# Second token product written by columns, with x and u turned by DMA, and six norms taken a segment earlier

## The chip, the cores and the metric

The kernel runs on one NeuronCore of one Trainium2 chip. The metric is the device time of one execution in microseconds (us). The unchanged kernel takes 398.41 us in the median of three runs (397.93, 398.41 and 399.13). A smaller number is better.

The core's engines each work through a queue of their own: PE (matrix products; PEld is its loading of the stationary operand), DVE (vector), ACT (scalar functions), POOL (a second, slower vector engine), and SP, which computes nothing and here issues most of the DMA transfers. Engines wait for each other through semaphores.

## The reference

Two layers follow each other. The first is cosine attention over 8 batches, 12 heads, 448 rows and 64 columns per head; the second is an MLP mixer over the attention's output x of shape 8 x 448 x 768.

```
q_n = q / (norm(q) + 1e-6);  k_n = k / (norm(k) + 1e-6)
scores = q_n @ k_n^T / tau
attn   = softmax(scores)                  # over keys
x      = attn @ v, heads side by side     # per batch 448 x 768

h   = relu(x^T @ w_tok1) @ w_tok2         # 768 x 256, then 768 x 448: over the rows (tokens)
u   = x + h^T                             # 448 x 768
h2  = relu(u @ w_ch1) @ w_ch2             # 448 x 1536, then 448 x 768: over the channels
out = u + h2
```

Inputs and output are float32. The kernel multiplies in float16 and accumulates in float32.

## The kernel before

**Tiles and stages.** Two heads form a pair; a batch has 6 pairs and the kernel 48 (0 to 47). A pair is 128 channels of x. The 448 rows of a batch are laid in four windows of 128 (the function windows): even batches use rows 0 to 447 and 64 rows of padding after them, odd batches use the last 128 rows first, so that 64 rows of padding lie in front.

For pair i the stages are: load_qk and load_v bring q, k and v; squares and sums give the sums of squares, norms turns them into 1/(norm + 1e-6) on ACT and DVE, scaled multiplies q and k by it on POOL (tile kq). From pair 12 on tpose_dma turns kq by a DMA transpose into qk; for earlier pairs tpose does this on PE. score multiplies qk (psS, psQ) and takes the exponential on ACT (pt). pv multiplies pt with v into psO, and DVE divides by the row sums into x (128 rows of a window x 4 windows x 128 channels). tok1 is the first token product: x against w1t gives psR, and DVE takes its maximum with 0 into rt (256 tokens by 128 channels). tok2 is the second token product: it gives psU, and DVE adds x to it into u16. udma turns u16 by a DMA transpose into ut, channels on partitions, which the channel products need. m_ch1 multiplies ut with wc1t (psG; relu on ACT into gt), and m_ch2 multiplies gt with wc2t (psF); DVE adds u16 to psF into ost, and SP stores ost.

**Order of the work.** The order is written out by hand. Pairs 0 to 6 have a prologue of their own. From i = 7 to 47 the main loop runs one step for each pair. In step i, PE scores pair i, applies the attention of pair i-1 (pv), takes one unit of channel work, finishes the scores, does tok2 of pair i-2, further units, and tok1 of pair i-1. A unit is one psG or psF group; refill puts a batch's units in a list when its pairs are done, and due spreads them over the steps. After the loop comes a tail with the last two tok2 and all units left.

The function side(i), called in each step after pv, queues the work of the other engines: load_qk six or seven pairs ahead, squares, cast_v, norms, scaled of pair i+2, tpose_dma of pair i+2 and load_v of pair i+4. SP therefore sees, step by step: the loads of q and k, the transpose of qk, the load of v, stores of finished ost tiles, and the transpose of u from tok2. It works them off in that order. For pairs 3 to 17 each pair's norms are taken alone, from pair 18 on three pairs together.

**Buffers.** The PSUM pool ps holds two tiles of tag b (psO, psR, psU and, below pair 12, the transposes of qk); ps2 holds three of tag s (psS, psQ, most psG and psF). x has three buffers, ut two (one for each of two batches in turn), u16 four.

Of the kernel before, what the change touches and what calls it, by code (L numbers as in the profile page):

```python
# [7 lines left out]
FP32 = mybir.dt.float32  # L8
# [14 lines left out]
def kernel(  # L23
# [145 lines left out]
    nc.gpsimd.memset(w1t[0:64, 4, :], 0.0)  # L169
    nc.gpsimd.memset(w2t[:, :, S:S + 64], 0.0)  # L170

# [80 lines left out]
    def sums_of(i):  # L252
        n, col, w = (-1 - i, 0, 1) if i < SINGLE else (i // HP, i % HP, HP)
        h = half.setdefault(n, {})
        if "ssq" not in h:
            tag = "" if w > 1 else "1"
            h["ssq"] = nrm.tile([128, w, 2 * QS], FP32, name=f"ssq_{i}", tag="ssq" + tag, bufs=4)
            h["rn"] = nrm.tile([128, w, 2 * QS], FP32, name=f"rn_{i}", tag="rn" + tag, bufs=4)
        return h, col
# [92 lines left out]
    def pv_rest(i):  # L352
        if old(i):
            return
        st = pipe[i]
        st["x"] = att.tile([128, 4, 128], FP16, name=f"x_{i}", tag="x", bufs=3)
        st["psO"] = [ps.tile([128, 4, E + 2], FP32, name=f"psO_{i}_{hh}", tag="b") for hh in range(2)]
        for m, lo in enumerate(windows(i // NPAIR)):
            for hh in range(2):
                hb = slice(hh * 64, hh * 64 + 64)  # L360
                at = 2 * S * KC + lo
                nc.tensor.matmul(st["psO"][hh][:, m, 0:E + 1], pts[i % 2][hb, at:at + 128],  # L362
                                 vts[(i // HP) % NV][hb, i % HP, 2 * KC, 0:E + 1], start=(m == 0), stop=False)

    def pv(i, hh):
        st = pipe[i]
        vt = vts[(i // HP) % NV]
        if old(i):
            if hh == 0:
                st["x"] = att.tile([128, 4, 128], FP16, name=f"x_{i}", tag="x", bufs=3)  # L370
# [15 lines left out]
    def tok1(i, wide=False):  # L386
# [8 lines left out]
        nc.vector.tensor_scalar_max(out=st["rt"][:], in0=psR[:], scalar1=0.0)  # L395

    def tok2(i, pe=False, wide=False):
        st = pipe[i]
        b, pj = i // NPAIR, i % NPAIR
        if pj == 0:  # L400
            u16[b] = mix.tile([128, DT, 4, 128], FP16, name=f"u16_{b}", tag="u16", bufs=4)
            ut[b] = mix.tile([128, DT, 4, 128], FP16, name=f"ut_{b}", tag="ut")
        psU = (ps2 if wide else ps).tile([128, 4, 128], FP32, name=f"psU_{i}", tag="s" if wide else "b")
        for m, lo in enumerate(windows(b)):
            for tt in range(TT):
                nc.tensor.matmul(psU[:, m], w2t[:, tt, lo:lo + 128], st["rt"][:, tt],  # L406
                                 start=(tt == 0), stop=(tt == TT - 1))
# [91 lines left out]

    SQ_AT = {12: [15, 16], 13: [17], 14: [18, 19], 15: [20]}  # L500
    SU_AT = {15: [18, 19]}

    with tc.manual_schedule():
# [116 lines left out]

        def side(i):
            single = i + 2 < SINGLE
            n = 6 if i < 2 * NPAIR else 7
            for t in range(i + n, i + (8 if i == 2 * NPAIR - 1 else n + 1)):
                if t < NP_ALL:
                    load_qk(t)
            for t in SQ_AT.get(i, [i + 3 if single else i + 5]):
                if t < NP_ALL:  # L630
                    squares(t)
            cast_v(i)
            if i in (8, 10):
# [12 lines left out]
            if i + 4 < NP_ALL:  # L646
                load_v(i + 4)

        for i in range(NPAIR + 1, NP_ALL):
# [39 lines left out]
        tok2(last)  # L689
# [38 lines left out]
```

## Time and profile before

The profiled execution took 395.4 us, of which 393.6 us are the span from its first to its last instruction; the three timed runs have a median of 398.41 us, 3.0 us above it.

| engine | busy us | share of the span | instructions |
|---|---|---|---|
| PE | 375.2 | 95% | 4132 |
| PEld | 243.5 | 62% | 4132 |
| DVE | 210.5 | 53% | 469 |
| ACT | 224.8 | 57% | 378 |
| POOL | 236.0 | 60% | 383 |

| group | count | mean ns of one |
|---|---|---|
| psU, tok2's product, 128 columns | 384 | 219 |
| psG, channel product 1, 448 columns | 576 | 352 |
| u <- psU, x on DVE, 128x512 | 48 | 691 (median) |
| ssq <- sq on DVE, one pair, 128x960 | 36 | 1143 |
| ut <- u, DMA transpose, issue on SP | 45 | 1241 (median) |
| qk <- kq, DMA transpose | 36 | landing 3.4 us after issue (median) |

Matrix products are pipelined: the mean of one contains its way through the array, and what one costs in a row is the distance from one start to the next. SP's rows show how long an issue holds the queue; the transfer itself goes on after it. The page counts SP's instructions as no work, so SP does not stand in the table of engines; it has to be read from the timeline of its queue. DMA queues: 117951 packets, 65.26 MB, q1 (SP) busy 67.6% of 16 engines over the span.

### The profile page before, as it was taken

Reading aid. Unit: us, or ns where it says so; the run is one execution under the profiler, and the core shown is the slowest. Engines: PE = TensorE matmul, PEld = TensorE weight load, DVE = VectorE, ACT = ScalarE, POOL = GpSimd, SP = SyncE. Lnnn points to the kernel's source line nnn. Section 1 sums busy time; section 2 is a strip of 40 time slices with the busy share of each in tenths; the row PEclk is TensorE's granted clock in tenths of the full one; section 3 lists DMA queues with packets and bytes.
Section 4 is the critical chain, followed back from the end, with each engine's and each line's share of the span. In section 5 each row is a group of like instructions: output and inputs, shape, how many; then the busy total and the mean of one; then the engine's idle time right before and its main releaser. Section 6 shows DMA issues by size and latency. Waiting matters only on the chain.

```text
span 393.6 us, 10211 instructions
## 1 busy us (share of the span) xinstructions
PE 375.2 (95%) x4132; PEld 243.5 (62%) x4132; DVE 210.5 (53%) x469; ACT 224.8 (57%) x378; POOL 236.0 (60%) x383
## 2 busy tenths in 40 slices
PE   5899899899999999999999999999999999999994
PEld 5567566476556666667656666667666666655562
DVE  6889767567544574465534574456534653421031
ACT  5899578665574547764574547755575536411400
POOL 6999887889777592939587592949484630000000
PEclk9899999999999999999999999999999999999999
DMA  8999999989787778896897688686786384022022
GB/s 213 260 234 205 243 260 195 219 216 218 177 201 172 156 182 213 161 174 177 176 220 165 156 213 202 159 176 146 183 187 132 91 158 68 15 65 83 0 81 81
DMA packets 117951, 65.26 MB, mean 166 GB/s; under 512 B 75920, under 2 KB 114320, under 8 KB 117904
## 3 DMA queue, kind: packets, MB, share of 16 engines
q1 hardware_dynamic: 113104, 58.71, 67.6%
q0 software_dynamic: 4080, 5.21, 7.7%
q10 hardware_dynamic: 720, 0.69, 0.6%
q8 instruction: 32, 0.52, 0.6%
q14 instruction: 15, 0.12, 0.1%
HBM read 43.45 MB, written 11.01 MB: 138 GB/s over the span
## 4 chain that ended last, share of the span: by engine, by line
PE 79%; POOL 6%; ACT 5%; DVE 5%; issue 2%; DMA 1%; POOLq 0%
PE psF L446 26%; PE psG L431 26%; PE psO L379 8%; PE psS L340 6%; PE psU L406 5%; PE psR L392 4%; ACT pt L341 3%; POOL kq L293 2%; PE psQ L347 2%; POOL sq L241 1%; DVE ssq L264 1%; PE psO L362 1%; POOL w1t L182 1%; DVE ost L450 1%; DMA qk<-kq 1%
## 5 line engine op out<-in xcount | busy, mean ns | idle before, releaser
L341 ACT ACTIVATE pt<-psS 128x896 f16<-128x896 f32 (+1 forms) x156 | 132.5, 917 | 57.8 <-PE psS L340 57.6
L431 PE MATMUL psG<-ut,wc1t 128*128 128x448 f16 x576 | 116.8, 352 | 0.8 <-ACT gt L434 0.8
L446 PE MATMUL psF<-wc2t,gt 128*128 128x384 f16 x672 | 115.9, 326 | 0.2 <-ACT gt L434 0.2
L446 PEld LDWEIGHTS <-gt 128*128 128x128 f16 x672 | 63.6, 98 | 39.0 <-issue 0.3
L434 ACT ACTIVATE gt<-psG 128x448 f16<-128x448 f32 x96 | 51.3, 543 | 60.9 <-PE psG L431 60.9
L293 POOL TENSOR_TENSOR kq<-kf,rn 128x384 f16<-128x384 f32 (+1 forms) x47 | 42.3, 899 | 70.8 <-ACT rn L281 62.0
L431 PEld LDWEIGHTS <-wc1t 128*128 128x128 f16 x576 | 53.9, 98 | 45.4 <-issue 1.1
L450 DVE TENSOR_TENSOR ost<-psF,u 128x384 f32<-128x384 f32 (+1 forms) x64 | 35.5, 554 | 63.6 <-PE psF L446 62.3
L264 DVE TENSOR_REDUCE ssq<-sq 128x15 f32<-128x960 f32 (+2 forms) x49 | 55.7, 1140 | 3.0 <-ACT sq L239 2.9
L395 DVE TENSOR_SCALAR rt<-psR 128x256 f16<-128x256 f32 x48 | 20.2, 420 | 62.6 <-PE psR L392 62.5
L293 POOL TENSOR_TENSOR kq<-qf,rn 112x512 f16<-112x512 f32 x45 | 47.0, 1044 | 3.0
L379 PE MATMUL psO<-vt,pt 128*128 128x65 f16 (+1 forms) x1248 | 48.3, 193 | 0.0
L379 PEld LDWEIGHTS <-pt 128*128 128x128 f16 (+1 forms) x1248 | 42.2, 97 | 5.1 <-issue 1.9
L340 PE MATMUL psS<-qk 64*128 64x448 f16 x312 | 41.3, 358 | 3.5 <-DMA qk<-kq 2.1
L383 DVE TENSOR_TENSOR x<-psO,rec 128x256 f16<-128x256 f32 x96 | 40.8, 425 | 3.3
L241 POOL TENSOR_TENSOR sq<-kf 128x384 f32<-128x384 f32 (+1 forms) x46 | 40.1, 872 | 1.9 <-DVE ssq L264 1.9
L241 POOL TENSOR_TENSOR sq<-qf 112x512 f32<-112x512 f32 x39 | 40.5, 1039 | 0.0
L409 DVE TENSOR_TENSOR u<-psU,x 128x512 f16<-128x512 f32 x48 | 33.0, 688 | 6.0 <-PE psU L406 4.4
L382 DVE RECIPROCAL rec<-psO 128x4 f32<-128x4 f32 x96 | 16.9, 176 | 29.0 <-PE psO L379 29.0
L406 PEld LDWEIGHTS <-w2t 128*128 128x128 f16 x384 | 24.6, 98 | 10.4 <-issue 3.3
L406 PE MATMUL psU<-rt,w2t 128*128 128x128 f16 x384 | 29.4, 219 | 1.7 <-DVE rt L395 1.1
L392 PEld LDWEIGHTS <-w1t 128*128 128x128 f16 x384 | 25.0, 98 | 8.2 <-DVE x L383 1.2
(55 smaller groups left out, 262.2 us busy)
## 6 DMA issues: line engine op xcount, KB each, us to landing
qf<-in_q_dram SPq DMA_DIRECT2D x48, 224.0 KB, 3.9
kf<-in_k_dram SPq DMA_DIRECT2D x36, 192.0 KB, 3.4
vf<-in_v_dram SPq DMA_DIRECT2D x36, 192.0 KB, 3.2
vf<-in_v_dram SPq DMA_DIRECT2D x12, 224.0 KB, 7.8
out_dram<-ost SPq DMA_DIRECT2D x8, 336.0 KB, 3.1
wc1t<-in_moe_w_ch_dram POOLq DMA_DIRECT2D x4, 576.0 KB, 10.2
wc2t<-in_moe_w_ch_dram POOLq DMA_DIRECT2D x2, 1152.0 KB, 10.7
out_dram<-ost SPq DMA_DIRECT2D x8, 288.0 KB, 2.9
```

The lines of the kernel that those rows point to most:

```text
L241: nc.gpsimd.tensor_mul(out=dst, in0=src, in1=src)
L264: nc.vector.tensor_reduce(out=h["ssq"][0:n, col, sl], in_=pipe[i]["sq"][0:n, sl], axis=AXX.X, op=ALU.add)
L293: eng.tensor_tensor(out=kq[0:p, a, 0:n].rearrange("p c g e -> p g c e"), in0=st["kq"[a]][:].rearrange("p (g c) e -> p g c e", g=2), in1=_b ...
L340: nc.tensor.matmul(psS[:, hh, 0:S], qk[hb, c * n:c * n + 128], qm[hb], start=True, stop=True)
L341: nc.scalar.activation(out=pts[i % 2][0:n, 2 * S * c:2 * S * (c + 1)].rearrange("p (h s) -> p h s", h=2), in_=psS[0:n, :, 0:S], func=AF.Ex ...
L379: nc.tensor.matmul(psO[:, m, 0:E + 1], pts[i % 2][0:n, at:at + 128], vt[0:n, i % HP, nch * hh + c, 0:E + 1], start=(old(i) and c == 0), st ...
L383: nc.vector.tensor_tensor(out=st["x"][:, :, hh * E:(hh + 1) * E], in0=psO[:, :, 0:E], in1=_bcast_free(rec[:], E), op=ALU.mult)
L392: nc.tensor.matmul(psR[:, tt], w1t[:, w1[m], tt * 128:(tt + 1) * 128], st["x"][:, m], start=(m == 0), stop=(m == 3))
L406: nc.tensor.matmul(psU[:, m], w2t[:, tt, lo:lo + 128], st["rt"][:, tt], start=(tt == 0), stop=(tt == TT - 1))
L431: nc.tensor.matmul(psG[:, 0:S], wc1t[:, dt, ct * 128:(ct + 1) * 128], ut[b][:, dt].rearrange("p m s -> p (m s)")[:, lo:lo + S], start=(dt ...
L434: nc.scalar.activation(out=gt[:, ct, (b % 2) * S:(b % 2 + 1) * S], in_=psG[:, 0:S], func=AF.Relu)
L446: nc.tensor.matmul(psF[:, 0:DH], gt[:, ct, lo:lo + 128], wc2t[:, ct, dh * DH:(dh + 1) * DH], start=(ct == 0), stop=(ct == CT - 1))
```

## The change

From batch 1 on (pairs 6 to 47, 42 of them) tok2 multiplies the other way round: rt is the stationary operand and all 448 columns of w2t stream past it, two products of 448 columns in place of eight of 128. psU then has channels on partitions, as ut has, so DVE adds and writes straight into ut. For that x must be turned too: the new function xdma turns x into xt by a DMA transpose, issued in side(i) for pair i-1 right after the loads of q and k. The transpose that used to turn u16 into ut now turns ut into u16, which only the last addition reads. ut becomes two fixed tiles, whose 64 columns of padding are set to zero once; w2t gets 64 more columns in front for the odd batches, and place_w2 one more copy. x goes from three buffers to two, ssq and rn of the threefold norms from four to three.

In steps 9 to 14 the sums and norms of pairs 12 to 17 are taken in the step three pairs ahead, after the last scores and before tok2, where they stood in the following step; scaled and tpose_dma of these pairs then stand first in the step's POOL and SP work (after xdma). squares are listed one step earlier to feed this. The tail issues xdma of the last pair and takes one unit more before the last tok2.

```diff
-    w2t = cst.tile([128, TT, S + 64], FP16, name="w2t")
+    w2t = cst.tile([128, TT, S + 128], FP16, name="w2t")
...
     def place_w2():
-        nc.gpsimd.tensor_copy(out=w2t[:, :, 0:S].rearrange("p t (c s) -> p t c s", c=NCH),
-                              in_=w2n[:].rearrange("p t (s c) -> p t c s", c=NCH))
+        w2c = w2n[:].rearrange("p t (s c) -> p t c s", c=NCH)
+        nc.gpsimd.tensor_copy(out=w2t[:, :, 64:S + 64].rearrange("p t (c s) -> p t c s", c=NCH), in_=w2c)
+        nc.gpsimd.tensor_copy(out=w2t[:, :, 0:64], in_=w2c[:, :, NCH - 1, SC - 64:SC])
...
+    uts = [cst.tile([128, DT, 4, 128], FP16, name=f"ut{i}") for i in range(2)]
+    for i in range(2):
+        nc.gpsimd.memset(uts[i][:, :, 3 - 3 * i, 64 - 64 * i:128 - 64 * i], 0.0)
...
+    def xdma(i):
+        st = pipe[i]
+        st["xt"] = att.tile([128, 4, 128], FP16, name=f"xt_{i}", tag="xt", bufs=2)
+        nc.sync.dma_start_transpose(out=st["xt"][:], in_=st["x"][:].rearrange("p m d -> p (m d)"))
...
     def tok2(i, pe=False, wide=False):
...
-            ut[b] = mix.tile([128, DT, 4, 128], FP16, name=f"ut_{b}", tag="ut")
+            ut[b] = uts[b % 2]
+        if i >= NPAIR:
+            lo = 64 * (b % 2)
+            psU = ps.tile([128, 512], FP32, name=f"psU_{i}", tag="b")
+            for tt in range(TT):
+                nc.tensor.matmul(psU[:, 0:S], st["rt"][:, tt], w2t[:, tt, 64 - lo:64 - lo + S],
+                                 start=(tt == 0), stop=(tt == TT - 1))
+            nc.vector.tensor_tensor(out=ut[b][:, pj].rearrange("p m s -> p (m s)")[:, lo:lo + S], in0=psU[:, 0:S],
+                                    in1=st["xt"].rearrange("p m s -> p (m s)")[:, lo:lo + S], op=ALU.add)
+            nc.sync.dma_start_transpose(out=u16[b][:, pj], in_=ut[b][:, pj].rearrange("p m s -> p (m s)"))
+            return
...
-    SQ_AT = {12: [15, 16], 13: [17], 14: [18, 19], 15: [20]}
-    SU_AT = {15: [18, 19]}
+    SQ_AT = {9: [12, 13], 10: [14], 11: [15], 12: [16], 13: [17], 14: [18], 15: [19, 20]}
...
         def side(i):
...
-            for t in SQ_AT.get(i, [i + 3 if single else i + 5]):
+            xdma(i - 1)
+            if i > 9 and single:
+                scaled(i + 2)
+                tpose_dma(i + 2)
+            for t in SQ_AT.get(i, [i + 3 if single else i + 5])[0:1]:
                 if t < NP_ALL:
                     squares(t)
             cast_v(i)
...
-            if single:
+            for t in SQ_AT.get(i, [])[1:]:
+                squares(t)
+            if i < 10:
                 norms(i + 2, i + 3)
                 norms(i + 2, i + 3, dve=True)
-            elif i + 4 < NP_ALL:
+                scaled(i + 2)
+            elif not single and i + 4 < NP_ALL:
...
-            if i + 2 < NP_ALL:
+            if not single and i + 2 < NP_ALL:
                 scaled(i + 2)
-                if i + 2 >= DMA_T0:
-                    tpose_dma(i + 2)
+                tpose_dma(i + 2)
...
                 score_rest(i)
+            if 9 <= i and i + 3 < SINGLE:
+                sums(i + 3)
+                norms(i + 3, i + 4)
+                norms(i + 3, i + 4, dve=True)
             if i > NPAIR + 1:
                 tok2(i - 2)
...
-            if i + 2 < SINGLE:
-                for t in SU_AT.get(i, [i + 3]):
-                    sums(t)
+            if i < 9:
+                sums(i + 3)
+            elif i + 3 == SINGLE:
+                sums(i + 3)
+                sums(i + 4)
...
+        xdma(last)
         tok2(last - 1)
         unit()
         tok1(last)
         unit()
+        unit()
         tok2(last)
```

More of the change, by code (lines that the diff above doesn't have):

```diff
@@ L169 @@
     nc.gpsimd.memset(w1t[0:64, 4, :], 0.0)
-    nc.gpsimd.memset(w2t[:, :, S:S + 64], 0.0)
+    nc.gpsimd.memset(w2t[:, :, S + 64:S + 128], 0.0)
     def weights_tok1():
@@ L256, in sums_of @@
             tag = "" if w > 1 else "1"
-            h["ssq"] = nrm.tile([128, w, 2 * QS], FP32, name=f"ssq_{i}", tag="ssq" + tag, bufs=4)
-            h["rn"] = nrm.tile([128, w, 2 * QS], FP32, name=f"rn_{i}", tag="rn" + tag, bufs=4)
+            h["ssq"] = nrm.tile([128, w, 2 * QS], FP32, name=f"ssq_{i}", tag="ssq" + tag, bufs=3 + (w == 1))
+            h["rn"] = nrm.tile([128, w, 2 * QS], FP32, name=f"rn_{i}", tag="rn" + tag, bufs=3 + (w == 1))
         return h, col
@@ L355, in pv_rest @@
         st = pipe[i]
-        st["x"] = att.tile([128, 4, 128], FP16, name=f"x_{i}", tag="x", bufs=3)
+        st["x"] = att.tile([128, 4, 128], FP16, name=f"x_{i}", tag="x", bufs=2)
         st["psO"] = [ps.tile([128, 4, E + 2], FP32, name=f"psO_{i}_{hh}", tag="b") for hh in range(2)]
@@ L369, in pv @@
             if hh == 0:
-                st["x"] = att.tile([128, 4, 128], FP16, name=f"x_{i}", tag="x", bufs=3)
+                st["x"] = att.tile([128, 4, 128], FP16, name=f"x_{i}", tag="x", bufs=2)
             n, nch = SC, NCH
@@ L405, in tok2 @@
             for tt in range(TT):
-                nc.tensor.matmul(psU[:, m], w2t[:, tt, lo:lo + 128], st["rt"][:, tt],
+                nc.tensor.matmul(psU[:, m], w2t[:, tt, 64 + lo:64 + lo + 128], st["rt"][:, tt],
                                  start=(tt == 0), stop=(tt == TT - 1))
```

## The prediction

> **What bounds the kernel now.** First the page: how busy PE is, and what the chain that ended last consists of.
>
> ```profile
> span 393.6 us, 10211 instructions
> PE 375.2 (95%) x4132; PEld 243.5 (62%) x4132; DVE 210.5 (53%) x469; ACT 224.8 (57%) x378; POOL 236.0 (60%) x383
> PE 79%; POOL 6%; ACT 5%; DVE 5%; issue 2%; DMA 1%; POOLq 0%
> ```
>
> PE sets the pace. Then the chain in order of time over one step in the middle; columns are start, length, engine, tile, line, number.
>
> ```profile
> 203.31 1.14 PE psG L431 x6
> 204.44 0.19 PE psQ L347
> 204.63 0.45 PE psU L406 x8
> 205.08 3.41 PE psG L431 x18
> ```
>
> There is no gap: a psU group of eight 128-column products costs 0.45 us (56 ns each), six products of 448 columns cost 1.14 us (190 ns each). Starts in PE's timeline, compared with these rates, leave only some 5 us of stalls between 46 and 340 us. The largest, 1.9 us, stands before step 12's scores (77.49): PE waits for qk of pair 12, whose transpose was issued at 70.23 and landed 7.2 us later.
>
> What stands next to PE? No page row counts SP, so I read its queue's timeline (start, length of the issue), here with one long wait in it.
>
> ```profile
> 217.91 0.67 SPq L129 DMA_DIRECT2D qf<-in_q_dram  x1
> 218.62 0.50 SPq L111 DMA_DIRECT2D kf<-in_k_dram  x1
> 223.17 1.23 SPq L325 DMA_TRANSPOSE qk<-kq  x1
> 224.45 0.58 SPq L111 DMA_DIRECT2D vf<-in_v_dram  x1
> 225.13 1.20 SPq L415 DMA_TRANSPOSE ut<-u  x1
> 226.42 0.99 SPq L464 DMA_DIRECT2D out_dram<-ost  x2
> 227.47 0.49 SPq L129 DMA_DIRECT2D qf<-in_q_dram  x1
> 228.00 0.49 SPq L111 DMA_DIRECT2D kf<-in_k_dram  x1
> 228.54 1.30 SPq L119 DMA_DIRECT2D kr<-in_k_dram  x2
> 229.94 1.26 SPq L325 DMA_TRANSPOSE qk<-kq  x1
> ```
>
> Issues follow each other with about 0.05 us between; only before the transpose of qk does SP wait (4.05 us here, for POOL's scaled). Summed over 91 to 284 us (steps 14 to 40, the ones that still load q and k): 197 issues last 158.3 us, their small gaps 10.3 us, and twelve waits over 0.3 us make up 24.6 us, of 193. SP is 87% full there. The landing times of the u transposes, in 45 to 64 us and in 91 to 284 us, and the table of stages (DMA share and GB/s are its last columns):
>
> ```profile
> DMA to landing us min/median/max: 6.3/7.7/9.1
> DMA to landing us min/median/max: 2.5/3.1/4.8
> ```
>
> ```profile
> 46.00:82.00 36.00, 33.74 (x407) 21.29 (x408) 22.32 (x57) 26.30 (x46) 28.59 (x43) 1.00 1.17 236
> 91.00:284.00 193.00, 191.50 (x2115) 124.19 (x2114) 105.61 (x226) 115.27 (x193) 135.62 (x225) 1.00 0.81 180
> 330.00:345.00 15.00, 14.30 (x155) 9.00 (x154) 5.17 (x13) 7.05 (x12) 0.00 (x0) 1.00 0.10 19
> ```
>
> The DMA engines are overfull up to 82 us (share 1.17, slow landings), with room after it (0.81).
>
> **What the Trainium skill says.** "TensorE: Matmul & The Clock Gate", section "Wait — 56ns, not 53.3ns?": warm products start N/2.4 GHz + 2.5 ns apart, 55.8 ns for 128 columns and 189 for 448; the trace agrees (56 and 190). "Perfetto Trace Analysis", section "DMA Instruction — HWDGE (DVE, Sync)": the reported time of such a DMA begins when its semaphores are satisfied and ends when the sequencer is free for the next. So SP's rows are occupancy, and waits are the gaps; the 0.05 us between neighbours agree. "DMA: Bandwidth & Descriptors", section "Issuing engines are not separate DMA queues", calls issue time "usually small relative to the DMA itself"; here it is 1.24 of 3.1 us for a u transpose, so I don't use that. "PSUM — Partial Sum Buffer", section "Engine vs sequencer instructions": the vector queue is strictly first in, first out. So a DVE addition that waits for a transfer holds what is behind it.
>
> **The change part by part.**
>
> PE. Two products of 448 columns, 2 x 190 = 380 ns, replace 450 ns: 0.07 us for each of 42 pairs, 2.9 us at most, and only where PE sets the pace. In the 15 steps outside 14 to 40 that is 1.0 us.
>
> DVE. The addition shrinks from 512 to 448 columns (about 0.07 us); DVE is 53% busy: nothing. But it now also waits for xt, and behind it on DVE stand rt, ost of later units and the next x, for which PE waits through PSUM buffers.
>
> SP. The old u transpose is replaced one for one by that of ut into u16, which is needed only much later. xdma is new: 42 issues of the same shape as the u transposes, which take 1.24 us in the median and 1.35 in the mean in 91 to 284 us, plus 0.05 of gap. 27 of them fall there: 27 x 1.29 = 34.8 us, or 27 x 1.40 = 37.8. Even if every wait vanished, SP would lack 34.8 - 24.6 = 10.2 to 13.2 us. What may be late first? The transpose of qk is issued right behind xdma; now it lands (issue + 3.4) 2.2 to 7.2 us, mostly about 4, before its scores. So SP may fall about 4 us behind for nothing, after which each us that it lacks pushes the next score, and PE with it: 6.2 to 9.2 us. PE's saving there is lost in it. I take 7.6 us. Steps 41 to 47 load no q and k; SP has room again, but time lost isn't won back.
>
> DMA engines. In 330 to 345 us a share of 0.10 over 15 us moved 19 GB/s, 285 KB, which is 2.2 transposes of 131 KB: 0.7 us of all 16 engines each. Per step of 7.3 us that is 0.10 of share: 0.81 becomes 0.91, below the 1.17 reached earlier. Taken as nothing; at worst landings grow by 0.5 us, and the free 4 us shrink as much. Before 82 us it is 7 x 0.7 = 5 us more in a full system. xt of pairs 7 and 8, issued as soon as SP is free (53.4 and 61.6 us), would land 7.7 us later, at 61.1 and 69.3; the additions stand at 61.4 and 67.2, or later by the next item. From nothing to 2 us each: I take nothing.
>
> Norms earlier. In steps 9 and 10 sums (1.14), Ln and Exp on ACT (0.32 + 0.22) and the DVE pair (0.19 + 0.25) come before tok2's addition: DVE is free at 61.4 in step 9 now, then at about 63.6, and the addition ends at 64.2 in place of 62.1. The copy of qk for the next step (it is still turned on PE) stands behind it, and psR needs psU's buffer, as the turned qk holds the other. PE would start psR at 62.7 and waits until 64.2: 1.5 us, the same in step 10: +3.0. From step 11 on no qk is turned on PE, and the units behind psU cover the delay. The gain: the transpose of pair 12 goes out some 2 to 3 us earlier, behind xdma of pair 9, which ends the 1.9 us wait: -1.9. Earlier POOL work for pairs 12 to 17 has no price; POOL is 60% busy. The second copy in place_w2 and the memsets (0.2 us each for such shapes) lie beside a prologue that waits for ACT: nothing, at most 0.5.
>
> Tail. PE stalls of about 0.35 us each between 340 and 347.5 us; one more unit (1.1 us) between tok1 and the last tok2 covers one or two: -0.5. xt of the last pair (x at 343.6, landing 2.4 us in this quiet part) comes before its addition.
>
> Sum: -1.0 + 7.6 + 3.0 - 1.9 - 0.5 = +7.2. Profiled: 395.4 + 7.2 = 402.6. The median of the runs stood 3.0 above the profiled execution: 398.4 + 7.2 = 405.6.
>
> **The rivals.**
>
> Faster. SP takes xdma in its stride, because waits and slack give more than I think. The point: 24.6 + 4 = 28.6 us for 27 issues, 1.06 us each. If an xdma costs SP less, PE stays the bound and the change is worth -2.9 - 1.9 - 0.5 + 3.0 = -2.3, down to -5.3 if the delays of steps 9 and 10 don't occur: 393.1 to 396.1, middle 395. For it: waits are long where they occur, and the earlier scaled of pairs 12 to 17 frees SP. Against: even the shortest u transpose took 1.19 us, with a queue idle before it or not.
>
> Slower still. xt comes late and stops DVE. As SP falls behind, xdma of a pair lands one step later than it is wanted: x is ready 2.3 us into a step, the addition 4.35 us into the next, with a lag of 4 us and a landing of 3.1 it comes 1 to 3 us late. If that, and not the score, is what PE feels first, the free 4 us aren't there: 398.4 + 7.2 + 4 = 409.6, and with the early xt (2 x 2) up to 414. It decides once SP's lag at xdma passes some 2 us.
>
> No change. SP's lack is just covered, as by slacks of 7 us and issues of 1.19: 27 x 1.24 - 24.6 - 7 = 1.9, with +3.0 - 1.9 - 0.5 - 1.0: +1.5; 398 to 400.
>
> **How the numbers follow.** SP bound as summed 0.63 (own range 401 to 409.5), slower still 0.15 (409.5 to 415), no change 0.07, faster 0.15. About 0.3% (1.2 us) can be told from no change here. Faster 0.14, same 0.06, slower 0.80. Time 405.6. The range reaches down to 397 and up to 412: it leaves out most of the faster case and half of the slowest, about 0.2.
>
> **What would show it.** Right: SP's waits in 91 to 284 us fall from 24.6 us to a few; steps there lengthen from 7.3 us on average by some 0.3; PE's waits name the transpose of qk, or DVE's addition waits for xt. psU groups take 0.38 us. The stall at step 12 is gone, new ones of 1.5 us stand before psR in steps 9 and 10. Wrong: xdma rows well below 1.2 us, or SP still waiting 5 us every third step, with steps no longer than before.

## The result, and the profile after

The changed kernel takes 418.9 us in the median of four runs (417.32 to 423.15), the kernel before 398.17 us beside it: a ratio of 1.0549, 95% interval 1.0456 to 1.0641. It is slower by some 20.7 us; 405.6 us (397 to 412) were forecast. The sign and the queue were right, the size was not. Executions more than 1.5% above the fastest of their kernel are left out of all medians and ratios of the experiments (e2, e5, e8, e13, e17 and the kernel before have some); with them e2's median is the 400.65 us that a later expectation names.

The profiled execution after is the longest of its four (423.15 us, span 421.4), so its absolute numbers lie some 4 us above the median. Its page first:

```profile
span 421.4 us, 9851 instructions
PE 380.9 (90%) x3880; PEld 234.8 (56%) x3880; DVE 208.5 (49%) x469; ACT 225.4 (53%) x378; POOL 237.4 (56%) x386
PE 67%; DMA 11%; DVE 9%; ACT 5%; POOL 4%; issue 2%; DVEq 0%; POOLq 0%
L422 DVE TENSOR_TENSOR ut<-psU,xt 128x448 f16<-128x448 f32 x42 | 25.9, 617 | 35.3 <-DMA xt<-x 27.9
```

PE fell from 95% to 90% of its span, and from 79% to 67% of the chain that ended last; transfers took 11% of that chain (1% before). The last line is the new addition: 42 of them, 617 ns each, with 35.3 us of idle DVE ahead of them, 27.9 of these until xt landed. The waits over the whole span show three links, DVE waiting for xt, PE for DVE's addition, and PE for qk (columns: us in total, times, longest):

```profile
DVE ut L422 <- DMA xt<-x: 27.9, 13, 5.6
PE psG L454 <- DVE ut L422: 11.7, 8, 3.1
PE psS L346 <- DMA qk<-kq: 6.8, 2, 6.6
```

Between 95 and 330 us PE waits mostly for the addition and hardly for qk:

```profile
PE psG L454 <- DVE ut L422: 10.4, 6, 3.1
PE psS L346 <- DMA qk<-kq: 0.3, 1, 0.3
```

SP's timeline at the place where the kernel before had a hole of 4.05 us (its 217.91 to 229.94):

```profile
207.02 1.24 SPq L331 DMA_TRANSPOSE qk<-kq  x1
208.31 0.57 SPq L111 DMA_DIRECT2D vf<-in_v_dram  x1
208.94 1.26 SPq L119 DMA_DIRECT2D vr<-in_v_dram  x2
210.30 1.01 SPq L487 DMA_DIRECT2D out_dram<-ost  x2
211.41 1.27 SPq L424 DMA_TRANSPOSE u<-ut  x1
212.72 0.58 SPq L129 DMA_DIRECT2D qf<-in_q_dram  x1
213.35 0.45 SPq L111 DMA_DIRECT2D kf<-in_k_dram  x1
213.90 1.19 SPq L406 DMA_TRANSPOSE xt<-x  x1
```

There is no hole. From step 14 to step 41 SP now waits 1.8 us in all (25.3 before, same steps), its issues, as the rows of the timeline give them, fill 202.9 of 218.4 us (164.4 of 200.5 before), and each new transpose took 1.21 us on average. The chain in order of time shows what that does:

```profile
213.90 4.78 DMA xt<-x
...
218.77 0.64 DVE ut L422
219.41 0.04 issue
219.45 4.06 PE psG L454 x12
```

x of that pair was ready 2.6 us into its step; SP came to its transpose only 11.9 us after the step had begun, and it landed at 218.68. The addition had been waiting 4.50 us, with DVE idle as its queue works in order, PE 3.12 us for the buffer that psU held. Then twelve products took 4.06 us, where the same twelve had taken 2.43 us at 213.89. The view by stretches gives the granted clock (third number from the end) during these products and after them:

```profile
219.45:222.80 3.35, 3.35 (x10) 1.32 (x10) 0.00 (x0) 0.54 (x1) 3.18 (x6) 0.50 0.95 276
223.00:225.00 2.00, 2.00 (x35) 1.38 (x34) 0.42 (x1) 1.25 (x2) 1.31 (x3) 1.00 1.12 194
```

The Trainium skill, "TensorE: Matmul & The Clock Gate", Part 1, section "What's actually happening", says that after an idle window of about 3.4 us PE drops to half its clock. This trace agrees on the half clock and not on the length, and the measurement decides: the stall here was 3.12 us, and one of 2.01 us, which ended at 171.49, was followed by a clock of 0.52 over 2.1 us. Three such stretches of some 3.4 us lie between 168 and 320 us. At half clock a stretch costs at most half its length, so they took up to 5 us of this execution (an estimate from these numbers).

Earlier, the chain holds one long transfer:

```profile
72.18 13.20 DMA qk<-kq
85.38 0.05 issue
85.43 1.30 PE psS L346 x6
```

The transpose of qk of pair 12 was to gain from the change. It was issued at 72.18, held SP for 6.28 us by itself (SP's timeline; 1.23 before) and landed 13.2 us after its issue began. PE waited 6.6 us. The change alone doesn't make such an issue: in e14, which adds nothing here, the same transpose held SP for 5.33 us. The stages, and the landings of xt in 45 to 64 and in 95 to 318 us:

```profile
46.00:82.00 36.00, 29.52 (x325) 17.09 (x322) 19.66 (x51) 24.10 (x43) 29.03 (x44) 1.00 1.16 204
95.00:318.00 223.00, 208.00 (x2090) 126.62 (x2086) 110.30 (x237) 123.63 (x208) 147.41 (x244) 0.98 0.88 184
```

```profile
DMA to landing us min/median/max: 8.3/9.0/9.8
DMA to landing us min/median/max: 2.5/3.2/4.8
```

In the late stage the DMA engines had room (share 0.88) and a turned x landed 3.2 us after its issue. It was late because it was issued late.

To find where time is lost I compare when each step begins (its first scores on PE) with the profile of the kernel before, whose steps 7, 11, 14, 16 and 47 begin at 43.68, 70.16, 89.20, 103.95 and 333.78 us. That execution (395.40 us) lies 2.2 to 3.5 us under the medians of its kernel, so the delays come out that much larger than against a median. The labels e1 to e14 are the experiments of the next section. Delays in us, one profiled execution each:

| kernel | median us (before beside it) | step 7 | 11 | 14 | 16 | 47 |
|---|---|---|---|---|---|---|
| changed | 418.9 (398.2) | 0.5 | 3.3 | 10.4 | 12.9 | 28.1 |
| e1 columns only | 419.8 (398.0) | 3.9 | 5.2 | 11.0 | 11.6 | 26.0 |
| e2 norms only | 400.3 (398.0) | 0.1 | 2.1 | 0.6 | 4.8 | 4.8 |
| e3 turned, unread | 415.3 (398.0) | 0.3 | 0.3 | 7.6 | 9.2 | 20.2 |
| e4 v by POOL | 405.1 (398.0) | 3.0 | 6.2 | 8.7 | 12.6 | 11.7 |
| e5 from batch 2 | 409.2 (398.0) | 0.3 | 2.4 | 2.3 | 5.2 | 11.9 |
| e6 wide units | 418.3 (398.0) | -0.2 | 5.3 | 9.0 | 11.3 | 21.5 |
| e7 both cures | 407.1 (398.0) | -0.1 | 2.0 | 6.2 | 8.7 | 12.3 |
| e9 two small copies | 413.2 (397.6) | 0.5 | 0.5 | 5.8 | 6.9 | 17.8 |
| e10 three small copies | 434.3 (397.6) | 0.1 | 0.1 | 6.6 | 10.6 | 38.4 |
| e11 six early, unread | 403.2 (397.6) | 0.0 | 0.5 | 7.3 | 8.0 | 8.0 |
| e13 x last | 427.7 (398.9) | 3.8 | 9.1 | 10.9 | 13.7 | 34.8 |
| e14 memsets | 397.9 (398.9) | 0.3 | 0.3 | 4.1 | 4.3 | 4.2 |

The early columns vary by some 4 us from one execution to the next: e14 changes nothing in steps 11 to 14 and loses 3.9 us there in this one execution. For the early part I therefore lean on medians, for the late one (16 to 47) on both. The traces show where the early variation comes from. PE's stall before step 12 lasted 1.8 to 1.9 us in the kernel before, e12 and e15, and the granted clock stayed at 1.00. In ten profiles it lasted 2.5 us or longer (4.5 in e14, 5.3 in e3, 6.6 in the changed kernel), and in each of them a stretch of 3.4 to 10.2 us at a clock of 0.50 begins in it or right after it.

### The profile page after: what moved, and what is told of

It reads as the page before. It is cut to its first block, busy times and chain, and to the rows that moved or that the text cites. A ratio compares the mean times of both kernels' runs of the same rounds, so it can differ in the third digit from the quotient of the medians.

```text
span 421.4 us, 9851 instructions
## 1 busy us (share of the span) xinstructions
PE 380.9 (90%) x3880; PEld 234.8 (56%) x3880; DVE 208.5 (49%) x469; ACT 225.4 (53%) x378; POOL 237.4 (56%) x386
## 2 busy tenths in 40 slices
DMA packets 140797, 70.74 MB, mean 168 GB/s; under 512 B 98768, under 2 KB 137168, under 8 KB 140752
## 4 chain that ended last, share of the span: by engine, by line
PE 67%; DMA 11%; DVE 9%; ACT 5%; POOL 4%; issue 2%; DVEq 0%; POOLq 0%
PE psF L469 26%; PE psG L454 20%; PE psO L385 7%; DMA xt<-x 6%; PE psS L346 5%; PE psR L398 4%; DMA qk<-kq 3%; ACT pt L347 3%; PE psU L420 3%; DVE ssq L270 2%; DMA w2n<-in_moe_w_tok_dram 2%; DVE ost L473 2%; DVE ut L422 2%; POOL kq L299 1%; PE psO L368 1%
## 5 line engine op out<-in xcount | busy, mean ns | idle before, releaser
L454 PE MATMUL psG<-ut,wc1t 128*128 128x448 f16 x576 | 121.8, 360 | 12.6 <-DVE ut L422 11.7
L454 PEld LDWEIGHTS <-wc1t 128*128 128x128 f16 x576 | 55.6, 99 | 64.8 <-issue 18.7
L469 PEld LDWEIGHTS <-gt 128*128 128x128 f16 x672 | 64.5, 98 | 42.6 <-issue 1.2
L346 PE MATMUL psS<-qk 64*128 64x448 f16 x312 | 42.4, 364 | 9.1 <-DMA qk<-kq 6.8
L401 DVE TENSOR_SCALAR rt<-psR 128x256 f16<-128x256 f32 x48 | 20.2, 420 | 54.3 <-PE psR L398 54.2
L422 DVE TENSOR_TENSOR ut<-psU,xt 128x448 f16<-128x448 f32 x42 | 25.9, 617 | 35.3 <-DMA xt<-x 27.9
L398 PEld LDWEIGHTS <-w1t 128*128 128x128 f16 x384 | 25.9, 100 | 11.0 <-issue 3.7
L398 PE MATMUL psR<-x,w1t 128*128 128x128 f16 x384 | 30.2, 223 | 2.0 <-DVE ut L422 1.9
L354 ACT ACTIVATE pt<-psQ 128x448 f16<-128x448 f32 x36 | 19.4, 539 | 23.1 <-PE psQ L353 23.1
## 6 DMA issues: line engine op xcount, KB each, us to landing
wc1t<-in_moe_w_ch_dram POOLq DMA_DIRECT2D x4, 576.0 KB, 10.6
```

The lines of the kernel that those rows point to most:

```text
L346: nc.tensor.matmul(psS[:, hh, 0:S], qk[hb, c * n:c * n + 128], qm[hb], start=True, stop=True)
L398: nc.tensor.matmul(psR[:, tt], w1t[:, w1[m], tt * 128:(tt + 1) * 128], st["x"][:, m], start=(m == 0), stop=(m == 3))
L454: nc.tensor.matmul(psG[:, 0:S], wc1t[:, dt, ct * 128:(ct + 1) * 128], ut[b][:, dt].rearrange("p m s -> p (m s)")[:, lo:lo + S], start=(dt ...
L469: nc.tensor.matmul(psF[:, 0:DH], gt[:, ct, lo:lo + 128], wc2t[:, ct, dh * DH:(dh + 1) * DH], start=(ct == 0), stop=(ct == CT - 1))
```

## The experiments

**Each half of the change alone.** e1 keeps the columns and the turning and puts the norms back:

```diff
-    SQ_AT = {9: [12, 13], 10: [14], 11: [15], 12: [16], 13: [17], 14: [18], 15: [19, 20]}
+    SQ_AT = {12: [15, 16], 13: [17], 14: [18, 19], 15: [20]}
+    SU_AT = {15: [18, 19]}
...
-            if 9 <= i and i + 3 < SINGLE:
-                sums(i + 3)
-                norms(i + 3, i + 4)
-                norms(i + 3, i + 4, dve=True)
```

> The columns and the turning of x alone, with the norms, sums and transposes of pairs 12 to 17 in the order of the kernel before. If the whole loss comes from the new transposes (first from overfull DMA engines up to step 13, about 8 to 10 us, then from SP's full queue, about 17 us in the profiled execution), this kernel is within 2 us of the changed one: 416 to 421 us. If my prediction's step on the norms holds (+3.0 - 1.9 us), it is some 1 us faster than the changed one. If it is the earlier norms that bring the early loss (their transposes now meet the transposes of x), then it is 6 to 10 us faster than the changed one: 409 to 413 us.

419.75 us, 1.0526 (1.0441 to 1.0610): all of the loss is here. e2 is the opposite, the second token product and u's transposes as before, the norms early.

> The earlier norms alone: the second token product, its additions and the transposes of u are those of the kernel before, x isn't turned. By my prediction's steps: +1.5 us in each of steps 9 and 10, -1.9 us at step 12, +1.1 us in sum: 399 to 400 us. If the early loss comes from the norms: 404 to 408 us. If the earlier transposes only gain: 396 to 397 us.

400.28 us, 1.0056 (1.0025 to 1.0086), 2.3 us more than before; the 1.1 that my steps gave is at the lower end of the interval (1.0 to 3.4 us). In the profile steps 9 and 10 lose 1.4 and 0.7 us (1.5 each were forecast) and the stall at step 12 is gone, 2.0 us, as forecast, but the delay came out again in step 14. PE's timeline of e2 (start, length, idle before and its releaser):

```profile
92.04 0.60 PE L362 MATMUL psO<-vt,pt 64*128 64x65 f16 x8 [1.47 <-DVE u L409]
92.58 0.98 PE L379 MATMUL psO<-vt,pt 128*128 128x65 f16 x24
93.37 3.75 PE L446 MATMUL psF<-wc2t,gt 128*128 128x384 f16 x12
```

u's addition, behind the norms on DVE, still held psU's buffer when the next step's psO wanted it: 1.47 us. Then the twelve psF products took 3.75 us; another such group at 97.59 took 2.11. So the price of this stall was 1.5 + 1.6 us.

**Turned, but read by nobody.** In the kernel before, x is turned at the changed kernel's place into a tile that nothing reads.

```diff
+    def xdma(i):
+        st = pipe[i]
+        st["xt"] = att.tile([128, 4, 128], FP16, name=f"xt_{i}", tag="xt", bufs=2)
+        nc.sync.dma_start_transpose(out=st["xt"][:], in_=st["x"][:].rearrange("p m d -> p (m d)"))
...
+            xdma(i - 1)
             for t in SQ_AT.get(i, [i + 3 if single else i + 5]):
```

(The tile x has two buffers in place of three to make room; so it has in e11 below, which loses nothing after step 16.)

> The kernel before (all of it, rows and norms too), with the transposes of x added at the place where the changed kernel issues them, into a tile that nothing reads (and two buffers of x in place of three). SP and the DMA engines carry the same as in the changed kernel, but no DVE addition waits for xt. Theory of the prediction (SP falls behind, and the transposes of qk come late): the loss is nearly the same, 410 to 419 us. Theory that the lateness of xt, through the DVE addition and the buffer of psU, is what PE feels: the loss up to step 13 stays in part (qk of pair 12 is late with or without a reader, 4 to 6 us), the rest of 17 us is mostly gone: 402 to 408 us.

415.33 us, 1.0421 (1.0342 to 1.0500). 17.3 of the 20.7 us come without a reader, so the reader isn't needed for most of the loss. In the changed kernel SP's lack reaches PE through the addition; without a reader it reaches PE through qk, as the prediction had it. The waits of PE in 95 to 330 us in e3, where the kernel before has no entry of this kind at all:

```profile
PE psS L340 <- DMA qk<-kq: 13.5, 15, 1.6
```

**Relieving SP.** In the changed kernel v is loaded by POOL's queue from pair 11 on:

```diff
-            (nc.scalar if nm == "k" and i < 3 else nc.sync).dma_start(
+            (nc.scalar if nm == "k" and i < 3 else nc.gpsimd if nm == "v" and i > 10 else nc.sync).dma_start(
```

(and likewise the other two loads of v.)

> The changed kernel with the loads of v (from pair 11 on) and its rest rows issued by POOL's queue in place of SP's. That takes some 0.6 us a step (18 to 20 us between steps 14 and 40) from SP, more than the 10 to 13 us which it lacked; the DMA engines carry the same bytes. If SP's queue is the cause of the loss after step 14 (17 us): 402 to 406 us. If the DMA engines' load is the cause: within 2 us of the changed kernel. The stall before step 12 (6.6 us) should stay either way.

405.13 us, 1.0137 (1.0040 to 1.0235): 13.8 us less, with the same bytes. After step 16 nothing is lost any more; the delay falls from 12.6 to 11.7 us. SP's timeline has 21.6 us of waits again in steps 14 to 41. The row of the stage in e4 (98 to 302 us):

```profile
98.00:302.00 204.00, 199.77 (x2035) 123.02 (x2033) 107.48 (x232) 121.12 (x204) 169.96 (x275) 0.99 1.00 196
```

The DMA engines' share is 1.00 there, above the changed kernel's 0.88, and from step 16 on the kernel is still no slower than before. So the late loss is SP's time and not the DMA engines'. The Trainium skill, "DMA: Bandwidth & Descriptors", section "Issuing engines are not separate DMA queues", says that issuing from several engines saves only sequencer time, "usually small relative to the DMA itself". Here that time was worth 13.8 us.

**The dose.** The kernel before, with two or three copies of 4 KB a step where e3 has the transpose of x (the edit is against e3):

```diff
-        nc.sync.dma_start_transpose(out=st["xt"][:], in_=st["x"][:].rearrange("p m d -> p (m d)"))
+        for j in range(2):
+            nc.sync.dma_start(out=st["xt"][0:16, j], in_=st["x"][0:16, j])
```

> The kernel before with two small copies (16 rows of 256 bytes each, of x into a tile that nothing reads) in every step at the place of the transpose of x. They take SP's time and hardly any of the DMA engines'. If each takes SP about 0.5 us as a load of k does, a step has some 1.1 us more on SP, 27 x 1.1 = 30 us against 25 us of waits in steps 14 to 40. If SP's time alone makes the late loss, and the waits and slack of an undisturbed start are really there: 0 to 4 us, 398 to 402 us, SP's waits down to some 5 us. If the early loss is the DMA engines' (as I think), the stage up to step 16 loses under 2 us; if it is SP's there too, 4 us or more and 403 to 408 us.

> The same with three small copies: 27 x 1.6 = 43 us against 25 us of waits, so SP lacks some 18 us in steps 14 to 40. If SP's time alone makes the late loss: 12 to 18 us there, 410 to 416 us, with hardly a wait left on SP and the share of the DMA engines as in the kernel before. If it is what the transposes do in the DMA engines: within 3 us of the kernel before. Early (up to step 16): under 2 us if that loss is the DMA engines', 5 us or more if it is SP's.

413.16 us, 1.0371 (1.0326 to 1.0416), and 434.28 us, 1.0908 (1.0853 to 1.0963). Both lie above every range that I had named, for I had the copies too cheap: a step's two took 1.34 us in the mean, its three 2.1 (27 steps). Summed from SP's timelines over steps 14 to 41, added issues less vanished waits are 38.0 - 24.5 = 13.5 us in e3, 36.1 - 24.0 = 12.1 in e9, about 58 - 24.0 = 34 in e10. The stage grew by 11.1, 12.1 and 30.8 us. The stage rows of the kernel before and of e9 (DMA share and GB/s last):

```profile
89.00:290.00 201.00, 199.34 (x2198) 129.12 (x2199) 109.29 (x232) 120.92 (x204) 140.91 (x236) 1.00 0.81 183
```

```profile
95.00:307.00 212.00, 199.29 (x2186) 128.21 (x2187) 109.05 (x231) 120.44 (x203) 140.71 (x234) 1.00 0.73 170
```

With the DMA engines idler than before (0.73), the loss after step 14 is that of the transposes. What PE waits for in 95 to 330 us, in e9 and in e10:

```profile
PE psS L340 <- DMA qk<-kq: 11.3, 13, 1.5
```

```profile
PE psS L340 <- DMA qk<-kq: 27.2, 17, 3.2
```

**The early transposes.** e5 is the changed kernel with columns from batch 2 on; e11 is e3 with only the six transposes of pairs 6 to 11.

```diff
-        if i >= NPAIR:
+        if i >= 2 * NPAIR:
             lo = 64 * (b % 2)
...
-            xdma(i - 1)
+            if i - 1 >= 2 * NPAIR:
+                xdma(i - 1)
```

> The changed kernel with the columns from batch 2 on: pairs 6 to 11 keep the rows of the kernel before, so the six transposes of x in steps 7 to 12 aren't issued; SP's load after step 13 is unchanged. If these six transposes, in the stage where the DMA engines are overfull, cost the early loss (step 16 starts 12.9 us late in the changed kernel, 4.8 us with the norms alone), 6 to 8 us come back: 411 to 413 us. If SP also enters the later stage less behind, up to 4 more: 407 to 411. If the early loss comes from somewhere else: within 2 us of 418.9.

> The kernel before with the six transposes of x for pairs 6 to 11 alone (steps 7 to 12), read by nothing; no other pair is turned. If these six make the early loss of the unread version (9.2 us by step 16): 404 to 408 us, with no loss after step 16. If that loss needs what follows (the seventh and later transposes, SP's queue): 398 to 401 us.

e5: 409.18 us, 1.0272 (1.0194 to 1.0350), 9.7 us less than the changed kernel. e11: 403.2 us, 1.0117 (1.0065 to 1.0170), 5.6 us more than the kernel before by the medians (2.6 to 6.8 by the interval). These six issues cost about half as much as the other 35 of e3. In e11's profile nothing is lost after step 16. In e5's profile the late stage (step 16 to 47) costs 6.8 us in place of 15.2; in e3's, 11.0.

I expected the small copies to lose under 2 us early if the transposes' own work in the full DMA engines were the reason. They lost 5.8 and 6.6 us by step 14 in their profiles; e14, which adds nothing there, lost 4.1 in its one. By the medians e9 lost 15.6 us, of which 10.9 came after step 16 in its profile, so some 4.7 are left for the early part (an estimate). So it isn't the transposes' work alone. Nor is SP full in this stage: in steps 7 to 11 it waits 11.7 us in the kernel before and still 6.6 to 7.5 in e3, e11 and the changed kernel. Whether the place in SP's queue matters, e13 asks: the changed kernel with the transpose of x issued last in its step.

```diff
-            xdma(i - 1)
...
             if i + 4 < NP_ALL:
                 load_v(i + 4)
+            xdma(i - 1)
```

> The changed kernel with the transpose of x issued last in its step, behind the transpose of qk and the load of v, in place of ahead of them. SP's total is the same. If the loss comes from what stands behind the new issue in the queue (the transposes of qk first): the stall before step 12 goes (4 to 6 us less), and in steps 14 to 40 SP's lack shows as late xt instead: 408 to 416 us. If SP's total alone counts: 416 to 420 us. If xt becomes so late that DVE's addition stops PE in every step: 420 to 428 us.

427.67 us, 1.0744 (1.0671 to 1.0818), some 8 us slower still. The wait for qk is gone in 130 to 350 us, and these have come:

```profile
PE psG L454 <- DVE ut L422: 9.5, 5, 3.9
PE psR L398 <- DVE ut L422: 4.0, 2, 2.4
```

SP has 13 us of waits in steps 14 to 41, so it isn't even full: PE waits for DVE's addition, that for xt, and SP in turn for x and ut from DVE. Moving the issue to the end isn't a way out; it makes the additions later, which costs more. What precisely holds the early stage (issues that grow long, or SP's in-order queue beside slow landings) stays open.

**The buffer of psU.** Steps 22, 28 and 40 of the changed kernel lost 3.6, 4.8 and 4.6 us at one stroke. e6 gives their psG the scores' pool, so they needn't wait for psU.

```diff
             while due():
-                unit()
+                unit(True)
             tok1(i - 1)
```

> The changed kernel with every unit in the loop taking its PSUM from the scores' pool, not from the two buffers that psU uses, so no psG has to wait until DVE's addition for xt has emptied psU. In the profile of the changed kernel steps 22, 28 and 40, with several such units, lost 13 us of the 15 us after step 16. If that buffer is how the late xt reaches PE: the loss falls to that of the unread transposes plus the norms, some 415 to 417 us, and steps 22, 28 and 40 show no jump of 3 us or more. If it is SP's rate alone that counts: the jumps are spread differently and the time stays within 2 us of 418.9. If the scores' pool becomes the new bound: slower, 420 to 424.

418.28 us, 1.0507 (1.0415 to 1.0598): not to be told from the changed kernel. The three jumps are gone (0.9, 1.3 and 0.9 us). But my edit has a price of its own: PE waits in 130 to 350 us are these, and the wait for ACT's gt stands at the batch starts, some 0.95 us each (five of them; seen again in e12, e15 and e16 below).

```profile
PE psS L346 <- DMA qk<-kq: 6.7, 8, 1.4
PE psG L454 <- ACT gt L457: 3.3, 4, 0.8
```

The buffer is one way in which the late xt reaches PE; without it SP's lack comes out at the scores. What the buffer adds in all, up to the 4 to 5 us that my edit hides, this run can't say.

**Cures together, and the cure on the kernel before.** e7 joins e4 and e5; e8 is the kernel before with v by POOL's queue.

> Both cures together: columns from batch 2 on, and v loaded by POOL's queue from pair 11 on. If early loss (six transposes among overfull DMA engines) and late loss (SP's queue) are two separate causes, the cures add: 405.1 less 5 to 8 us, 397 to 400 us, that is the norms alone (400.65 us) less PE's saving of 0.07 us a pair (2.5 us). If they overlap: 402 to 405 us.

> The kernel before with v loaded by POOL's queue from pair 11 on, nothing else. SP waits 24.6 us of 193 there already, so if SP isn't what bounds it, nothing is gained: 397 to 400 us. If the qk transposes gain from a freer SP: 395 to 397. If the loads by POOL's queue cost the DMA engines more (their share from 160 to 290 us rose from 0.91 on average to 1.02 in the changed kernel with v by POOL's queue), it may be slower in the stage up to 100 us: 400 to 404.

e7 took 407.09 us, 1.0204 (1.0137 to 1.0272), where 397 to 400 was expected if the cures add; they don't. Two lines of its waits (of 44 to 130 and of 130 to 350 us) show where 6.6 us of it went: POOL's queue also loads the second channel weights, and PE now waited 3.5 us for these; and two products waited for psU's buffer.

```profile
PE psF L469 <- DMA wc2t<-in_moe_w_ch_dram: 3.5, 1, 3.5
PE psG L454 <- DVE ut L422: 3.1, 2, 2.2
```

e8 took 398.80 us, 1.0023 (1.0001 to 1.0045): freeing SP gives nothing in the kernel before, where PE is the bound.

**The prologue.** Step 7 starts 3.0 to 3.9 us late in the profiles of e1, e4, e12 and e13. DVE's timeline of e1 shows a multiplication of 3.66 us, which takes 0.69 or 0.70 us in all profiles without the delay:

```profile
12.41 3.66 DVE L299 TENSOR_TENSOR kq<-qf,rn 112x512 f16<-112x512 f32 x1
```

and POOL's timeline of e1 around it:

```profile
11.91 1.06 POOL L247 TENSOR_TENSOR sq<-kf 112x512 f32<-112x512 f32 x1
12.91 1.05 POOL L299 TENSOR_TENSOR kq<-kf,rn 112x512 f16<-112x512 f32 x1
13.90 0.61 POOL L223 CAST vt<-vf 112x512 f16<-112x512 f32 x1
14.48 1.04 POOL L247 TENSOR_TENSOR sq<-kf 112x512 f32<-112x512 f32 x1
```

The Trainium skill, "SBUF — State Buffer", section "Who interferes with whom", says that a DVE operation with two SBUF inputs contends with a GpSimd operation that reads SBUF, and that the order of issue decides who blocks. It fits: in the kernel before, POOL's square had ended (11.77) and DVE, starting at 12.27, took 0.69 us, while POOL's multiplication beside it took 1.55. In e1 POOL came 1.2 us later, its square still ran at 12.41, and DVE took until 16.07, through the POOL operations that followed too; that it stood through several is more than the page says. From 15.6 us on the granted clock was 0.50 for 6.8 us. The memsets of ut (0.77 us) are ahead of POOL's loads. e14 puts four memsets into the kernel before, e15 takes ut's out of a combined version:

```diff
     nc.gpsimd.memset(w2t[:, :, S:S + 64], 0.0)
+    for _ in range(4):
+        nc.gpsimd.memset(w2t[:, :, S:S + 64], 0.0)
```

> The kernel before with four more memsets of 128 x 128 (some 0.8 us, of bytes that are zeroed already) on POOL, where the changed kernel has its memsets of ut. If they bring the long DVE multiplication of the prologue: step 7 starts 3 to 4 us later in the profile when it occurs, and the median of the runs rises by 1 to 4 us, 399 to 402 us. If the long multiplication was chance, or needs the second copy of w2: 397 to 398.5 us, as before.

397.93 us, 0.9988 (0.9952 to 1.0024): no cost. POOL's square was 0.47 us later than before and ended at 12.24, just as DVE began; the collision wasn't reached. So the delay is seen in four of eight profiles with ut's memsets and in none of eleven without them, but no run brings it about by itself: its cause is argued, and its share of the median isn't settled.

**Can a version beat both?** e12: columns from batch 2, norms as before, all units in the scores' pool, v by POOL's queue from pair 19 on. e15: without ut's memsets. e16: and with the transpose of x last. e17: e15 with the units in their own buffers.

> A version meant to keep the gain and leave out the losses: columns from batch 2 on, norms in the order of the kernel before, every unit of the loop in the scores' pool, v loaded by POOL's queue from pair 19 on (after the second channel weights have been loaded by that queue). If the causes are the ones found (six early transposes, SP's queue, the order of the norms 2.6 us), what is left is PE's saving of 0.07 us for 36 pairs, 2.5 us: 395.5 to 398 us. If something else remains: 399 to 404 us.

> The combined version (columns from batch 2 on, norms as before, units in the scores' pool, v by POOL's queue from pair 19 on) without the memsets of ut, whose bytes are all written by the transposes of batches 0 and 1. If the memsets cost the prologue 3 to 4 us: 398 to 399 us, and the multiplication at 12.4 us takes 0.7 us. If not: 401 to 403 us.

> The same with the transpose of x issued last in its step. With v on POOL's queue SP has some 17 us of waits left in steps 14 to 40, so xt should be in time; the transposes of qk and then PE gain what they still lose. If the order on SP matters where SP isn't full: 396 to 398 us, equal to the kernel before or a little faster. If not: as e15. If xt comes too late for the addition: 401 us or more.

> The combined version without memsets (columns from batch 2 on, norms as before, v by POOL's queue from pair 19 on), with the units after the first two of a step in their own two buffers as in both kernels, not in the scores' pool. If the 0.95 us at each of five batch starts came from the scores' pool: 4 to 5 us less than that version, 395.5 to 397.5 us, a ratio of 0.99 to 0.998 to the kernel before. If psU's buffer holds psG up instead when xt is late (one such stall cost 4 us in the version with v by POOL's queue from pair 11 on): 399 to 402 us.

| version | us | ratio | 95% |
|---|---|---|---|
| e12 | 401.96 | 1.0104 | 1.0080 to 1.0128 |
| e15 | 401.23 | 1.0066 | 1.0042 to 1.0091 |
| e16 | 403.16 | 1.0123 | 1.0076 to 1.0171 |
| e17 | 398.68 | 1.0036 | 1.0004 to 1.0068 |

None is faster than the kernel before. e12, e15 and e16 fell into the ranges that I had named for a cure that fails, e17 1.2 us above its first range. The reason named for e16 isn't seen: no wait of PE for the addition stands in its profile from 44 to 350 us. In e12, e15 and e16 each of the five batch starts after step 16 costs about 0.95 us, from my own edit; in e15:

```profile
200.50 3.56 PE L452 MATMUL psG<-ut,wc1t 128*128 128x448 f16 x18 [0.84 <-ACT gt L455]
```

With the units in their own buffers that is gone, and so is about half of the difference to the kernel before. PE's saving of 0.07 us a step is then visible: in e17 the delay falls from 2.7 us (step 20) to 2.5 (step 23), in e4 from 12.62 (step 16) to 11.36 (step 38). It is not enough to win.

## Why the prediction was right or wrong

Differences of medians, each good to some 2 to 4 us, set beside the terms of the sum:

| term | predicted | measured |
|---|---|---|
| SP short in steps 14 to 40 | +7.6 | +11.8 (e3 less e11) |
| six transposes before 82 us | 0 | +5.6 (e11) |
| norms earlier, with step 12 | +1.1 | +2.3 (e2) |
| PE, tail, reading xt, prologue | -1.5 | +1.0 (what is left) |
| sum | +7.2 | +20.7 |

The parts don't add exactly: e1 and e2 alone make 21.8 + 2.3 = 24.1 us, and the changed kernel, with both, 20.7.

**Right.** That SP's queue, and no engine, becomes the bound after step 14, which e4 and the two doses of small copies show; an issue of 1.2 us per transpose; SP's waits falling to a few us; late qk and late xt as what PE feels. A psU group takes 0.37 us (213.52 to 213.89, start to start), as forecast. The tail gained 0.3 us in the changed kernel, of the 0.5 forecast.

**Wrong: "SP may fall about 4 us behind for nothing".** This is the term that was sized 7.6 and measured 11.8. I read the slack (2.2 to 7.2 us) inside 91 to 284 us and took it as there at the start. Without it my sum was 10.2 to 13.2, and e3 lost 11.0. The profile of the kernel before had the warning at the entry of the stage, on PE's timeline:

```profile
89.20 0.74 PE L340 MATMUL psS<-qk 64*128 64x448 f16 x6 [0.17 <-DMA qk<-kq]
```

At step 14 PE already waited for qk: no slack to spend. The traces let the slack be followed, as the time between the landing of a pair's qk and its first score. In the kernel before it is 0.0 and 0.2 us at pairs 14 and 15 and only then grows to some 4 us (3.9 to 4.9 at pairs 17 to 19). In e3 it never grows: 0.6 to 2.0 us at pairs 17 to 20, nothing at pairs 21 to 23. Where the early transposes are left out and the norms are early (e5), it is there, 3.0 to 5.4 us at pairs 16 to 21, and it is spent at pair 25 (0.0). From step 16 on e5 lost 6.8 us, e3 11.0: the difference is about that slack. Each is one profiled execution, and e5 differs from e3 in more than the slack, so the size is supported and not pinned down. In steps 14 and 15 e5 lost 2.9 us more, with PE waiting for DVE (1.6 and 0.7 us) and not for qk.

**Wrong: "From nothing to 2 us each: I take nothing".** I asked only when xt of pairs 7 and 8 would land, and not what stood behind their issues. Behind them stood the transpose of qk of pair 12, whose score was already 1.9 us late. Six issues cost 5.6 us, where I had put nothing. The range of that step should have come from this row and not from xt's own landing. How the six hold qk up is the part that stays open.

**Wrong: "From step 11 on ... the units behind psU cover the delay".** In e2 the delay of u's addition came out in step 14, 1.47 us, and the products behind it took 1.6 us longer (clock 0.54 from 93.4 to 97.0 us). I had priced all stalls at their length.

**The gain at step 12** (-1.9) came in e2 and was lost in the changed kernel to the new transposes (6.6 us of wait at the same place).

**The prologue**, priced at nothing, at most 0.5, cost 3 to 4 us in four of the eight profiles with ut's memsets.

**The rivals.** "Slower still" named xt's lateness, with a lag that decides from some 2 us. That working was wrong: by its own figures a step of 7.3 us, plus 4.35, less 2.3 and 3.1, leaves some 6 us of lag free. The lag was 9.3 us at the place shown, and from 95 us on xt's lateness was the path by which PE felt SP's lack. But e3 shows that a missing reader would have spared little, so it was mostly a second outlet for the same lack and not an addition. "Faster" needed xdma below 1.06 us on SP; it took 1.21. "No change" needed slacks that weren't there.

## What to carry to other kernels

A queue that issues transfers is an engine: add up its issues and waits by stage, as for PE, and count a new issue against the waits that are left where it stands, and not against the average. Slack is a stock that can be spent once; look at the entry of the stage whether it is still there. A stall of PE can cost more than its length: after stalls of 1.47, 2.01 and 3.12 us the clock was at half for some 3.4 us, which cost about 1.6 us more; after one of 1.9 us (step 12 of the kernel before) and one of 1.59 us (e5) it stayed full. And work on POOL that moves by a microsecond may come to lie beside a DVE operation that then takes 3.7 us in place of 0.7.

## What the runs showed of the hardware that I had not expected

- On SP a copy of 4 KB took 0.67 us to issue, a transpose of 128 x 512 half-precision values 1.2 to 1.4 us: two tiny copies block the queue as long as one transpose.
- While the DMA engines were overfull, an issue itself grew: 6.28 us for one transpose of qk, 4.36 us for one of u, against 1.19 to 1.25.
- One DVE multiplication grew from 0.69 to between 3.3 and 3.8 us beside POOL's work.
- With v loaded by POOL's queue, and the same 70.74 MB, the DMA engines were busier in the stage: a share of 1.00 over 204 us (e4) in place of 0.88 over 223 us, that is 204 against 196 us of all 16 engines.
- In all ten profiles with a stall of 2.5 us or longer before step 12 the granted clock fell to 0.50 for 3.4 to 10.2 us; in the three with 1.8 to 1.9 us it didn't.
